# Three fused layers on one Trainium2 core: a first mixture whose TensorE order is written out, loads and splits in another order, and plain units weighed inside their additions

## The chip, the cores and the metric

The kernel runs on one core of a Trainium2 chip, all in fp32. The metric is the device time in microseconds (us) of one execution, lower is better. A core has a matrix engine (TensorE, PE in the profile; its weight loads are PEld), VectorE (DVE), ScalarE (ACT), GpSimd (POOL), and SyncE (SP), which here issues the large loads. Each engine works through its own queue in order; semaphores order the engines against each other.

## The reference

```python
# attention with a memory: B, H, S, D = 4, 8, 576, 64
scores = where(causal, -1e9, q @ k.T / sqrt(D)); a = softmax(scores)
q_p = where(q > 0, q, exp(q) - 1) + 1
mem_out = (q_p @ M_prev) / (q_p @ z_prev + 1e-6)
x = g * mem_out + (1 - g) * (a @ v)            # g from beta; x is 2304 x 512
# first mixture: 8 experts of 4 slots each
logits = x @ phi                               # 2304 x 32
slot_input = softmax(logits, axis=0).T @ x     # 32 x 512
for e in range(8):
    slot_out[e] = relu(slot_input[e] @ w1[e]) @ w2[e]      # 4 x 512 -> 4 x 1024 -> 4 x 512
x = softmax(logits, axis=1) @ slot_out
# second mixture: 8 experts over all rows, dense
P = exp(x @ w_gate - max); 8 rounds of row and column balancing of P
out = sum over e of P[:, e:e+1] * (relu(x @ w1[e]) @ w2[e])
```

## The kernel before

**Splitting.** Wherever TensorE multiplies in its fast form, an fp32 operand is split into a rounded part ("h", written by ScalarE) and a remainder ("l", operand minus rounded part, written by VectorE or GpSimd), and a product is three matmuls: h by h, h by l, l by h.

**Attention (0 to 257 us).** Sixteen pairs of heads, one after the other. Per pair the queries and keys are loaded split by head (`qd`, `kd`, two copies of 64 rows) and once more as a plain 128-row tile for the memory features (`qp`, `load_q1`); `qh`, `kh` and the remainders (`pre_ql`, `klz`) are made from `qd` and `kd`, and the features phi(q) = max(q, 0) + min(exp(q), 1) from `qp`. Then scores, row maxima, exponentials, transposes and the product with v. SyncE's queue issues the loads in the order in which the code calls them. What stands where on the engines in this stage is decided by the tile scheduler from costs, not written out.

**First mixture (273 to 316 us).** The x rows and the slot softmax are done by then. `sT` holds the 32 slot inputs; the weights come as 32 tiles `wm` of 1 MiB, 16 for layer 1 and 16 for layer 2. A block is four experts by 512 hidden columns: four `wm` tiles, each used by four 32-column matmuls (L830) into one bank `ph`, then a Relu into `h1`, then four transposes `phT` (L839) into `hT`. Layer 2 (L848) runs the same way over eight tiles a group into `pso`; `so` is its copy (L854, VectorE, 128x512) and `psT` its four transposes (L857) into `soT`, which is x's slot output for everything behind it. The combine weights c of one batch of rows are transposed with each block (`pc`, L809). The order on TensorE in this stage too is the scheduler's.

**Entry to the second mixture (316 to 324.5 us).** x is never formed: it is c times the 32 rows `soT`. `prepare_a` (L999, `pa`) multiplies soT by w1 of an expert; `spread_a` and `layer1` (L1052, `l`) give the hidden values of 256 rows (a "unit") at a time; `split_h` splits them into `a11`, `a21`, `a12`, `a22` (ACT L1082, DVE L1089). `w_hi` and `w_lo` (L963, L969) split the halves `raw` of w2 into BB1 and BB2, h and l. `gate_weights` writes `gsel`, with which `gate_scores` (L1159, `pgl`) makes the logits of the gate.

**Second mixture (324.5 us to the end).** Six plain units g = 0 to 5 (L1336) for expert 0, without the gate's weight since the gate is still being balanced (`balance_rows`, `sum_columns`, `balance_columns`); their results wait in `accA`, `accB`, `accD`. Then 66 units g = 6 to 71 in Strassen form: expert e and unit u from 0 to 8, seven products p1 to p7 each (L1369 to L1371), with sums `s1` to `s4` split beside them. The weights of each expert carry the gate's weight c from then on. The six plain units have to be multiplied by their gate weight `Pr` before expert 1 is added to them (units g = 9 to 14): `settle` does that with four VectorE multiplications per unit in g = 6 to 11. From 273 us's end on, that is from the entry to the second mixture, the order on PE, DVE, ACT and POOL is the order of the code: side work has a slot 7u + k, set by the tables `beside` and `at`, and is issued behind product k of unit u.

## Time and profile before

| | us |
|---|---|
| median of three runs | 1150.27 (1144.68 to 1154.06) |
| the profiled execution | 1150.16 |
| its span from first to last instruction | 1148.4 |
| TensorE matmuls busy | 1093.7 (95%) |
| VectorE, ScalarE, GpSimd busy | 873.3, 640.9, 659.4 |

The span is what the profile shows; the execution's own time is 1.8 us longer. Times of rows count from the span's start. Busy time of PE is modelled: matmuls overlap one another, so a row's duration is longer than the distance to the next.

### The profile page before, as it was taken

The numbers are of one execution on the slowest core, as the hardware profiler recorded it, in microseconds if no ns is written. First come the engines' busy times: TensorE is split into PE (matmuls) and PEld (weight loads), VectorE is DVE, ScalarE is ACT, GpSimd is POOL, SyncE is SP. The second block draws the span as 40 slices with busy tenths as digits, with TensorE's granted clock in tenths as the row PEclk, the third lists the DMA queues.
The fourth block names the chain that finished last, engine by engine and source line by source line (L and its number), as shares of the span: only waits on it lengthen the run. The fifth ranks groups of instructions, "written<-read, shape, count | busy, mean of one in ns | idle before, by whom it ended". The sixth has DMA issues, their size and how long they took to land.

```text
span 1148.4 us, 24410 instructions
## 1 busy us (share of the span) xinstructions
PE 1093.7 (95%) x9191; PEld 990.3 (86%) x9191; DVE 873.3 (76%) x1894; ACT 640.9 (56%) x1385; POOL 659.4 (57%) x602
## 2 busy tenths in 40 slices
PE   5899999998999999999999999999999999999998
PEld 4677777773377888899999999999999999999998
DVE  6788888875036568878778877877887887788876
ACT  6888878761233366455645644555464565456542
POOL 5333333300324287568767867786885777678665
PEclk9999999997989999999999999999999999999999
DMA  6677777338922003100400320130031013000111
GB/s 162 191 207 221 204 220 203 92 108 359 372 74 92 1 2 129 38 1 4 145 20 1 111 56 1 37 116 16 1 132 35 1 45 112 11 2 3 54 56 56
DMA packets 42789, 106.01 MB, mean 92 GB/s; under 512 B 8240, under 2 KB 18608, under 8 KB 38576
## 3 DMA queue, kind: packets, MB, share of 16 engines
q1 hardware_dynamic: 42240, 104.37, 28.4%
q8 instruction: 73, 1.20, 0.4%
q14 instruction: 44, 0.36, 0.1%
q10 hardware_dynamic: 432, 0.09, 0.0%
HBM read 96.04 MB, written 4.72 MB: 88 GB/s over the span
## 4 chain that ended last, share of the span: by engine, by line
PE 76%; DVE 14%; ACT 6%; issue 2%; DMA 1%; POOL 0%; SPq 0%; DVEq 0%; ACTq 0%
PE y L1369 16%; PE y L1371 16%; PE y L1370 16%; PE y L1336 5%; PE l L1052 5%; PE po L436 3%; DVE f L1076 2%; PE ph L830 2%; ACT sm L360 2%; PE pt L399 2%; PE pa L999 1%; PE pso L848 1%; DVE sm L356 1%; PE pc L1236 1%; PE pma L449 1%
## 5 line engine op out<-in xcount | busy, mean ns | idle before, releaser
L1076 DVE SCALAR_TENSOR_TENSOR f<-l,f 128x512 f32<-128x512 f32 x264 | 181.3, 687 | 57.4 <-ACT a11h L1082 49.4
L1093 POOL TENSOR_TENSOR s1l<-f,s1h 128x512 fp32r<-128x512 f32 x66 | 88.6, 1342 | 153.3 <-ACT s1h L1082 149.3
L1385 DVE TENSOR_TENSOR accA<-accA,y 128x512 f32<-128x512 f32 (+1 forms) x129 | 86.6, 671 | 41.1 <-PE y L1371 37.6
L1082 ACT ACTIVATE a12h<-l 128x512 fp32r<-128x512 f32 x72 | 43.3, 601 | 98.6 <-PE y L1371 82.3
L1093 POOL TENSOR_TENSOR s4l<-f,s4h 128x512 fp32r<-128x512 f32 x66 | 86.2, 1306 | 19.6 <-PE y L1370 10.4
L1385 DVE TENSOR_TENSOR accB<-accB,y 128x512 f32<-128x512 f32 x129 | 88.3, 685 | 5.0
L1093 POOL TENSOR_TENSOR s3l<-f,s3h 128x512 fp32r<-128x512 f32 x66 | 86.0, 1303 | 2.0 <-ACT s3h L1082 2.0
L1052 PE MATMUL l<-c4T,a 128*128 128x256 f32 x576 | 80.0, 282 | 6.9 <-DVE a22l L1089 6.0
L1093 POOL TENSOR_TENSOR s2l<-f,s2h 128x512 fp32r<-128x512 f32 x66 | 86.2, 1307 | 0.0
L360 ACT ACTIVATE sm<-sm,mn 128x128 f32<-128x128 f32 (+3 forms) x128 | 71.1, 556 | 19.6 <-DVE mn L356 17.9
L1052 PEld LDWEIGHTS l<-c4T,a 128*128 128x128 f32 x576 | 72.5, 190 | 9.9 <-DVE a22l L1089 8.3
L1072 ACT ACTIVATE f<-l 128x512 f32<-128x512 f32 x66 | 39.0, 592 | 72.8 <-PE l L1052 71.9
L1369 PE MATMUL y<-T2h,s2h 128*128 128x256 f32 x264 | 76.4, 289 | 0.0
L1369 PE MATMUL y<-T1h,s1h 128*128 128x256 f32 x264 | 73.4, 278 | 1.5 <-DVE accA L1385 1.5
L1369 PE MATMUL y<-BB1h,a11h 128*128 128x256 f32 x264 | 73.4, 278 | 1.1 <-DVE accB L1385 1.1
L969 POOL TENSOR_TENSOR BB1l<-raw,BB1h 128x512 fp32r<-128x512 f32 x32 | 41.1, 1300 | 57.8 <-ACT BB1h L963 53.6
L1370 PE MATMUL y<-BB2l,s4h 128*128 128x256 f32 x264 | 73.5, 278 | 0.4 <-DVE BB2l L969 0.3
L1369 PE MATMUL y<-BB2h,a12h 128*128 128x256 f32 x264 | 73.7, 279 | 0.0
L1371 PE MATMUL y<-BB1h,s3l 128*128 128x256 f32 x264 | 73.3, 278 | 0.1
L1370 PE MATMUL y<-T2l,s2h 128*128 128x256 f32 x264 | 73.3, 278 | 0.0
L1371 PE MATMUL y<-T2h,s2l 128*128 128x256 f32 x264 | 73.2, 277 | 0.0
L1371 PE MATMUL y<-BB1h,a11l 128*128 128x256 f32 x264 | 73.1, 277 | 0.0
(314 smaller groups left out, 4221.7 us busy)
## 6 DMA issues: line engine op xcount, KB each, us to landing
wm<-in_moe_w_dram SPq DMA_DIRECT2D x32, 1024.0 KB, 8.1
raw<-in_moe_w_dram SPq DMA_DIRECT2D x32, 512.0 KB, 3.9
w<-in_moe_w_dram SPq DMA_DIRECT2D x32, 512.0 KB, 4.3
qd<-in_q_dram SPq DMA_DIRECT2D x30, 288.0 KB, 4.3
kd<-in_k_dram SPq DMA_DIRECT2D x30, 288.0 KB, 4.5
qp<-in_q_dram SPq DMA_DIRECT2D x16, 288.0 KB, 3.6
vt<-in_v_dram SPq DMA_DIRECT2D x16, 256.0 KB, 2.8
out_dram<-accB SPq DMA_DIRECT2D x18, 128.0 KB, 1.8
```

The costliest lines, as they stand in the source:

```text
L360: nc.scalar.activation(out=sm[:, 0:n], in_=sm[:, 0:n], func=AF.Exp, scale=-1.0, bias=mnc, accum_out=X.sums[:, i, h : h + 1],)
L969: eng(g).tensor_tensor(out=w_tile(e, nm, "l")[:, h], in0=full(e, nm, i), in1=w_tile(e, nm, "h")[:, h].bitcast(F32), op=ALU.subtract,)
L1052: nc.tensor.matmul(ph[:, f, :], a4s[e][:, P * (KH * j + f) : P * (KH * j + f) + P], c4T[:, UT * u : UT * u + UT], start=True, stop=True,)
L1072: nc.scalar.activation(out=f_tile(g, nm), in_=ph(g, nm), func=AF.Relu)
L1076: nc.vector.scalar_tensor_tensor(out=f_tile(g, nm), in0=ph(g, src), scalar=0.0, in1=b, op0=ALU.max, op1=op)
L1082: nc.scalar.activation(out=h_tile(g, nm, "h"), in_=ph(g, nm) if a else FU[g, nm], func=AF.Relu if a else AF.Copy)
L1093: nc.gpsimd.tensor_tensor(out=lo, in0=FU[g, nm], in1=hi, op=ALU.subtract)
L1336: nc.tensor.matmul(Y[g, i], X[g, f"a{i}{j}", "hhl"[n]][:, f, :], BB[j, "hlh"[n]][:, f].rearrange("p a c -> p (a c)"), start=j == 1 and f = ...
L1369: nc.tensor.matmul(o_, hh[:, f, :], wh[:, f, :], start=f == 0, stop=False)
L1370: nc.tensor.matmul(o_, hh[:, f, :], wl[:, f, :], start=False, stop=False)
L1371: nc.tensor.matmul(o_, hl[:, f, :], wh[:, f, :], start=False, stop=f == KH - 1)
L1385: nc.vector.tensor_tensor(out=acc, in0=acc, in1=y, op=ALU.add)
```

## The change

1. **First pair.** The plain load `qp` of pair 0 is left out. Its features come from the split queries `qd`: two Exp on ScalarE and two maxima on VectorE, 64x576 each, in place of one Exp and one Relu of 128x576 on ScalarE. SyncE issues pair 1's queries, the memory, pair 1's keys and then v, where it issued `qp`, v, memory, queries, keys. In pair 1 one of the two query remainders moves from GpSimd to VectorE.
2. **First mixture.** TensorE's order is written by hand: layer 1 of a block runs whole, and the transposes of the block before stand behind it. Layer 2 of a group is in two halves, with transposes between them. The copy `so` is half VectorE, half ScalarE.
3. **Loads.** The four tiles of w1 are issued behind two of the four halves `raw` instead of behind all four.
4. **Splits of BB2.** The splits of B21 and B22 stand behind `a11`, `a21` and ahead of `gate_weights`; one of the two remainders of each moves from GpSimd to VectorE.
5. **Expert 1.** `prepare_a` two slots and `split_a`, `move_a` one slot later.
6. **Plain units.** `settle` is gone. For expert 1 and u below 6 the addition into `accB`, half of `accA` and `accD` multiplies by `Pr` as it adds (`weigh`).

```diff
         def load_q1(p):
             X = pairs[p]
             X.qp = e0.tile([P, NT * P], F32, tag="qp", name="qp", bufs=CFG["qpb"])
+            if p == 0:
+                return
...
         load_q1(0)
+        load_heads(1, "qd")
+        load_memory(0)
+        load_heads(1, "kd")
         load_v(0)
-        load_memory(0)
-        load_heads(1, "qd")
-        load_heads(1, "kd")
...
-                e or CFG["e_ql"][h], X.qh[sl, h, c0:c1], X.qd[sl, h, c0:c1], X.qh[sl, h, c0:c1]
+                e or ("DP" if X.p == 1 else CFG["e_ql"])[h], X.qh[sl, h, c0:c1], X.qd[sl, h, c0:c1], X.qh[sl, h, c0:c1]
...
+            if X.p == 0:
+                for h in range(2):
+                    sl = slice(D * h, D * h + D)
+                    nc.scalar.activation(out=X.qe[sl], in_=X.qd[sl, h], func=AF.Exp)
+                    nc.vector.tensor_scalar(
+                        out=X.qp[sl, 0:S], in0=X.qd[sl, h], scalar1=0.0, scalar2=None, op0=ALU.max
+                    )
...
+            if n:
+                so[g] = b2.tile([P, DM], F32, tag="so", name="so", bufs=1)
+                nc.vector.tensor_copy(so[g][:, 0:256], pso[g][:, 0:256])
+                nc.scalar.activation(out=so[g][:, 256:], in_=pso[g][:, 256:], func=AF.Copy)
...
+        with tc.manual_schedule(engines={mybir.EngineType.PE}):
+            c4 = combine(0)
+            first(0)
+            for bb in range(1, B):
+                first(bb)
+                first_t(bb - 1)
+                combine_t(bb - 1, c4)
+                c4 = combine(bb)
+            second(0, 0)
+            first_t(B - 1)
+            second(0, 1)
+            second(1, 0)
+            second_t(0)
+            second(1, 1)
+            combine_t(B - 1, c4)
+            second_t(1)
...
-    for u in range(RAW):
-        for i in range(4):
-            at(6 + u, 3 + i, settle, u, i)
...
+        def weigh(acc, T):
+            nc.vector.scalar_tensor_tensor(
+                out=acc, in0=acc, scalar=Pr[:, 2 * u + T, 0:1], in1=y, op0=ALU.mult, op1=ALU.add
+            )
...
-        if nm == "p5":
+        plain_before = e == 1 and u < RAW
+        if nm == "p5" and plain_before:
+            weigh(B_[:, 0:CW], 0)
+            weigh(B_[:, CW:], 1)
+        elif nm == "p5":
             put(halves(B_), both(y))
-        elif nm == "p1" and e == 1 and u < RAW:
+        elif nm == "p1" and plain_before:
             put(A[:, 0:CW], y, True)
-            put(A[:, CW:], y)
+            weigh(A[:, CW:], 0)
+        elif nm == "p7" and plain_before:
+            weigh(D_, 1)
...
-    load_raw(0)
+    load_raw(0, (0,))
     load_w1(0, 1)
+    load_raw(0, (1,))
...
-        for nm in ("B11", "B12", "B21", "B22"):
+        for nm in ("B11", "B12"):
             for i in range(2):
                 w_hi(0, nm, i)
                 w_lo(0, nm, i, "P")
...
         split_h(0, "a21")
+        for nm in ("B21", "B22"):
+            for i in range(2):
+                w_hi(0, nm, i)
+                w_lo(0, nm, i, "PD"[i])
         gate_weights()
```

How the instructions stand is shown at three places. The first is TensorE between the first two blocks of the first mixture, before: `ph_3940` is the second block's bank, `wm4` to `wm7` its tiles, `phT` and `pc` the transposes of the first block's hidden values and of the combine weights.

```order
L809 MATMUL pc_3912<-ident_67,c4_3890 128x128 x4
L809 MATMUL pc_3918<-ident_67,c4_3890 128x64
L830 MATMUL ph_3940<-wm4_1590,sT_65 32x512
L839 MATMUL phT_3921<-ident_67,h1_3910 128x128 x4
L830 MATMUL ph_3940<-wm4_1590,sT_65 32x512 x3
L830 MATMUL ph_3940<-wm5_1803,sT_65 32x512 x4
L830 MATMUL ph_3940<-wm6_2018,sT_65 32x512 x4
L830 MATMUL ph_3940<-wm7_2255,sT_65 32x512 x4
```

The same place on TensorE after the change, where `ph_3917` is the second block's bank.

```order
L841 MATMUL ph_3917<-wm4_1591,sT_65 32x512 x4
L841 MATMUL ph_3917<-wm5_1804,sT_65 32x512 x4
L841 MATMUL ph_3917<-wm6_2019,sT_65 32x512 x4
L841 MATMUL ph_3917<-wm7_2256,sT_65 32x512 x4
L852 MATMUL phT_3936<-ident_67,h1_3915 128x128 x4
L820 MATMUL pc_3942<-ident_67,c4_3895 128x128 x4
L820 MATMUL pc_3948<-ident_67,c4_3895 128x64
L841 MATMUL ph_3964<-wm8_2497,sT_65 32x512 x4
```

The single `ph` matmul that stood alone between two sets of transposes has joined the other three of its tile, and both sets of transposes now stand behind the whole block.

The second place is VectorE at the first unit's splits, before.

```order
L1089 SCALAR_TENSOR_TENSOR a11l<-l_4281,a11h 128x512
L1089 SCALAR_TENSOR_TENSOR a21l<-l_4281,a21h 128x512
L1147 TENSOR_TENSOR gsel<-pg,gsel 32x8 x2
L1150 TENSOR_TENSOR gsel<-ident 128x32
L1089 SCALAR_TENSOR_TENSOR a12l<-l_4276,a12h 128x512
L1089 SCALAR_TENSOR_TENSOR a22l<-l_4276,a22h 128x512
```

The same on VectorE after, where `raw_4223` and `raw_4225` are the second tiles of B21 and B22.

```order
L1125 SCALAR_TENSOR_TENSOR a11l<-l_4279,a11h 128x512
L1125 SCALAR_TENSOR_TENSOR a21l<-l_4279,a21h 128x512
L1005 TENSOR_TENSOR BB2l<-raw_4223,BB2h 128x2x256
L1005 TENSOR_TENSOR BB2l<-raw_4225,BB2h 128x2x256
L1183 TENSOR_TENSOR gsel<-pg,gsel 32x8 x2
L1186 TENSOR_TENSOR gsel<-ident 128x32
L1125 SCALAR_TENSOR_TENSOR a12l<-l_4274,a12h 128x512
```

Two remainders now stand ahead of `gsel` on VectorE. On ScalarE at the same place it is the four rounded parts of BB2, after the change:

```order
L1171 ACTIVATE soB<-soT 128x512
L1118 ACTIVATE a11h<-l_4279 128x512
L1118 ACTIVATE a21h<-l_4279 128x512
L999 ACTIVATE BB2h<-raw_4223 128x2x256 x2
L999 ACTIVATE BB2h<-raw_4225 128x2x256 x2
L1180 ACTIVATE gsel<-pg 128x8
L1118 ACTIVATE a12h<-l_4274 128x512
```

Before, `gsel` stood right behind `a21h` there; the four `BB2h` stood ahead of `ahi`, some rows earlier.

The third place is VectorE between units g = 9 and g = 10 (expert 1, u = 0 and 1), before.

```order
L1385 TENSOR_TENSOR accB<-accB,y_5564 128x512
L1221 TENSOR_TENSOR cP<-Cw,Pr 128x128
L1231 TENSOR_TENSOR c_5622<-cP,chi 128x4x64
L1385 TENSOR_TENSOR accA<-accA,y_5594 128x256
L1076 SCALAR_TENSOR_TENSOR f<-l_5612,f 128x512 x2
L1385 TENSOR_TENSOR accD<-accD,y_5627 128x256
L969 TENSOR_TENSOR BB2l<-raw_4783,BB2h 128x2x256
L1279 TENSOR_SCALAR accA<-accA,Pr 128x256
L1076 SCALAR_TENSOR_TENSOR f<-l_5607,f 128x512
L1089 SCALAR_TENSOR_TENSOR a11l<-l_5612,a11h 128x512
L1279 TENSOR_SCALAR accB<-accB,Pr 128x256
L1385 TENSOR_TENSOR accA<-accA,y_5655 128x512
```

The same place on VectorE after.

```order
L1415 SCALAR_TENSOR_TENSOR accB<-accB,Pr,y_5558 128x256 x2
L1257 TENSOR_TENSOR cP<-Cw,Pr 128x128
L1267 TENSOR_TENSOR c_5617<-cP,chi 128x4x64
L1415 SCALAR_TENSOR_TENSOR accA<-accA,Pr,y_5588 128x256
L1112 SCALAR_TENSOR_TENSOR f<-l_5606,f 128x512 x2
L1415 SCALAR_TENSOR_TENSOR accD<-accD,Pr,y_5622 128x256
L1005 TENSOR_TENSOR BB2l<-raw_4789,BB2h 128x2x256
L1112 SCALAR_TENSOR_TENSOR f<-l_5601,f 128x512
L1125 SCALAR_TENSOR_TENSOR a11l<-l_5606,a11h 128x512
L1411 TENSOR_TENSOR accA<-accA,y_5650 128x512
```

The multiplications L1279 between the sums `f` and the splits `a` are gone; the one addition of 128x512 into `accB` has become two of 128x256, and those into `accA` and `accD` keep their number.

## Rows read from the trace of the kernel before

**Rows 1.** Window, attention: length, busy us (count) of PE PEld DVE ACT POOL, PEclk, DMA.
```profile
31.50:257.00 225.50, 207.82 (x1866) 168.67 (x1864) 195.05 (x686) 180.38 (x485) 67.98 (x109) 1.00 0.63 184
```

**Rows 2.** Windows: a piece, units 6 to 12, units 15 to 21; columns as above.
```profile
412.50:425.00 12.50, 11.43 (x96) 10.92 (x95) 10.97 (x14) 7.25 (x15) 12.50 (x10) 1.00 0.00 1
408.73:499.79 91.06, 81.88 (x695) 78.13 (x694) 76.67 (x118) 51.16 (x102) 64.05 (x50) 1.00 0.16 53
520.64:598.96 78.32, 78.32 (x696) 77.09 (x695) 63.29 (x104) 43.81 (x84) 57.64 (x46) 1.00 0.19 62
```

**Rows 3.** Waits of PE from 408.73 to 499.79: total us, times, longest.
```profile
PE l L1052 <- DVE a22l L1089: 5.5, 6, 1.2
PE y L1369 <- DVE accA L1385: 1.5, 2, 1.2
```

**Rows 4.** Line L1279, settle: duration ns min/median/max, first and last start.
```profile
L1279 DVE TENSOR_SCALAR accB<-accB,Pr x12: 335/640/1449, 419.0 to 488.2; 128x256 f32<-128x256 f32 x12
L1279 DVE TENSOR_SCALAR accA<-accA,Pr x6: 537/1265/1475, 416.4 to 483.3; 128x256 f32<-128x256 f32 x6
L1279 DVE TENSOR_SCALAR accD<-accD,Pr x6: 339/1352/1416, 424.1 to 489.6; 128x256 f32<-128x256 f32 x6
```

**Rows 5.** Groups of DVE from 408.73 to 499.79: count, busy us, mean ns.
```profile
L1385 DVE TENSOR_TENSOR accB<-accB,y 128x512 f32<-128x512 f32 x11 | 7.4, 676 | 0.1
...
L1385 DVE TENSOR_TENSOR accD<-accD,y 128x256 f32<-128x256 f32 x10 | 4.1, 409 | 0.0
```

**Rows 6.** Timeline of PE, one block of the first mixture: start, length.
```profile
284.42 0.86 PE L809 MATMUL pc<-ident,c 128*128 128x128 f32 x5
285.21 1.05 PE L830 MATMUL ph<-wm,sT 128*32 128x512 f32 x2
286.18 0.66 PE L839 MATMUL phT<-ident,h 128*128 128x128 f32 x4
286.77 3.63 PE L830 MATMUL ph<-wm,sT 128*32 128x512 f32 x30
290.33 0.86 PE L809 MATMUL pc<-ident,c 128*128 128x128 f32 x5
```

**Rows 7.** Timeline, end of the first mixture: start, length, idle before and what ended it.
```profile
305.67 2.43 ACT L963 ACTIVATE BB1h<-raw 128x512 fp32r<-128x512 f32 x4 [8.01 <-DMA raw<-in_moe_w_dram]
...
307.12 7.07 PE L848 MATMUL pso<-wm,hT 128*32 128x512 f32 x64
...
308.37 2.29 ACT L963 ACTIVATE BB2h<-raw 128x512 fp32r<-128x512 f32 x4 [0.27 <-DMA raw<-in_moe_w_dram]
...
315.10 0.63 PE L857 MATMUL psT<-ident,so 128*128 128x128 f32 x4 [0.91 <-DVE so L854]
...
316.05 1.93 PE L999 MATMUL pa<-w,soT 128*32 128x256 f32 x32 [0.32 <-DVE soT L858]
```

**Rows 8.** Timeline behind the first layer1: the splits, gsel and pgl.
```profile
324.56 0.60 ACT L1082 ACTIVATE a21h<-l 128x512 fp32r<-128x512 f32 x1 [0.76 <-DVE a11l L1089]
...
325.89 0.34 DVE L1147 TENSOR_TENSOR gsel<-pg,gsel 32x8 fp32r<-32x8 f32 x2
...
327.66 1.48 PE L1159 MATMUL pgl<-gsel,c4T 128*128 128x40 f32 x12
```

**Rows 9.** Tile BB2l on DVE: duration ns min/median/max.
```profile
L969 DVE TENSOR_TENSOR BB2l<-raw,BB2h x7: 1462/1470/1552, 457.0 to 1057.9; 128x512 fp32r<-128x512 f32 x7
```

**Rows 10.** Windows in which the granted clock is half.
```profile
24.01:30.84 6.83, 6.09 (x27) 4.06 (x29) 1.38 (x8) 4.63 (x13) 3.25 (x5) 0.50 0.05 13
...
320.97:327.80 6.83, 6.71 (x25) 6.04 (x25) 2.67 (x7) 2.35 (x5) 0.00 (x0) 0.50 0.57 231
```

**Rows 11.** Timeline of PE at expert 1's prepare_a.
```profile
349.98 1.93 PE L999 MATMUL pa<-w,soT 128*32 128x256 f32 x32 [1.42 <-DVE cs L1207]
```

**Rows 12.** Timeline, first pairs: the remainders on POOL and PE's wait.
```profile
20.20 2.63 POOL L258 TENSOR_TENSOR qh<-qd,qh 64x512 fp32r<-64x512 f32 x2
...
22.88 0.44 PE L354 MATMUL ps<-kh,qh 128*128 128x128 f32 x2 [2.30 <-POOL qh L258]
```

More of the change, by code (lines that the diff above doesn't have):

```diff
@@ L306, in pre_exp @@
             X.qe = e5.tile([P, S], F32, tag="sc", name="qe")
[L307 to L308 removed]
+            if X.p == 0:
[5 more added lines that the diff above has]
+                    )
+            else:
+                nc.scalar.activation(out=X.qe, in_=X.qp[:, 0:S], func=AF.Exp)
+                nc.scalar.activation(out=X.qp[:, 0:S], in_=X.qp[:, 0:S], func=AF.Relu)
             nc.gpsimd.memset(X.qp[:, S:], 0.0)
@@ L816, in combine_t @@
                 )
-        hTs = []
-        for g in range(E // 4):
-            hT = b2.tile([P, KF, 4 * SPE + 32 - SPE], F32, tag="hT", name="hT")
+        hTs = [b2.tile([P, KF, 4 * SPE + 32 - SPE], F32, tag="hT", name="hT") for _ in range(2)]
+        for hT in hTs:
             nc.gpsimd.memset(hT[:, :, 4 * SPE :], 0.0)
-            hTs.append(hT)
-            for n in range(FF // 512):
-                bb = FF // 512 * g + n
-                c4 = combine(bb)
-                ph = ps_h.tile([P, 512], F32, tag="h", name="ph")
-                for c in range(KD):
-                    for j in range(4):
-                        e = SPE * (4 * g + j)
-                        nc.tensor.matmul(
-                            ph[32 * j : 32 * j + 32, :], sT[:, c, e : e + 32], wm[1, g, n, c][:, j, :],
-                            start=(c == 0), stop=(c == KD - 1),
-                        )
-                h1 = b2.tile([P, 512], F32, tag="h1", name="h1", bufs=1)
-                nc.scalar.activation(out=h1, in_=ph, func=AF.Relu)
-                combine_t(bb, c4)
-                pt = ps_m.tile([P, 512], F32, tag="m", name="phT")
-                for c in range(4):
-                    nc.tensor.transpose(pt[:, P * c : P * c + P], h1[:, P * c : P * c + P], ident)
-                nc.vector.tensor_copy(
-                    hT[:, 4 * n : 4 * n + 4, 0 : 4 * SPE].rearrange("p c (j s) -> p c j s", j=4),
-                    pt.rearrange("p (c j s) -> p c j s", c=4, j=4)[:, :, :, 0:SPE],
-                )
@@ L844, in infini_attention_soft_moe_sinkhorn_moe, with first @@
-        for g in range(E // 4):
-            pso = ps_g.tile([P, 512], F32, tag="g", name="pso")
-            for f in range(KF):
+        NN = FF // 512
+        h1s, pso, so = {}, {}, {}
+        def first(bb):
+            g, n = divmod(bb, NN)
+            ph = ps_h.tile([P, 512], F32, tag="h", name="ph")
+            for c in range(KD):
+                for j in range(4):
+                    e = SPE * (4 * g + j)
+                    nc.tensor.matmul(
+                        ph[32 * j : 32 * j + 32, :], sT[:, c, e : e + 32], wm[1, g, n, c][:, j, :],
+                        start=(c == 0), stop=(c == KD - 1),
+                    )
+            h1 = h1s[bb] = b2.tile([P, 512], F32, tag="h1", name="h1", bufs=1)
+            nc.scalar.activation(out=h1, in_=ph, func=AF.Relu)
@@ new lines, in first_t, with second @@
+        def first_t(bb):
+            g, n = divmod(bb, NN)
+            pt = ps_m.tile([P, 512], F32, tag="m", name="phT")
+            for c in range(4):
+                nc.tensor.transpose(pt[:, P * c : P * c + P], h1s[bb][:, P * c : P * c + P], ident)
+            nc.vector.tensor_copy(
+                hTs[g][:, 4 * n : 4 * n + 4, 0 : 4 * SPE].rearrange("p c (j s) -> p c j s", j=4),
+                pt.rearrange("p (c j s) -> p c j s", c=4, j=4)[:, :, :, 0:SPE],
+            )
+        def second(g, n):
+            if n == 0:
+                pso[g] = ps_g.tile([P, 512], F32, tag="g", name="pso")
+            for f in range(KF // 2 * n, KF // 2 * n + KF // 2):
@@ L914, in w_tile, with load_raw @@
         return W[e, nm, z]
-    def load_raw(e):
-        for r, c in ((0, 0), (0, 1), (1, 0), (1, 1)):
+    def load_raw(e, rows=(0, 1)):
+        for r, c in ((r, c) for r in rows for c in (0, 1)):
             t = rawq[e, r, c] = mC.tile([P, KH, CW], F32, tag=f"raw{r}{c}", name=f"raw{r}{c}")
@@ L1273, in add_u @@
         eng(g[1]).tensor_tensor(out=D_, in0=D_, in1=A[:, 0:CW], op=ALU.add)
-    def settle(u, i):
-        A, B_, D_ = accA[:, u], accB[:, u], accD[:, u]
-        t, T = ((A[:, CW:], 0), (B_[:, 0:CW], 0), (B_[:, CW:], 1), (D_, 1))[i]
-        nc.vector.tensor_scalar(
-            out=t, in0=t, scalar1=Pr[:, 2 * u + T, 0:1], scalar2=None, op0=ALU.mult
-        )
     def at(u, k, f, *args):
```

16 lines of the change are left out of this document (7 added, 9 removed).

## The prediction

> **What bounds the kernel now.** I read the busy time by stage first, then PE's waits in the stages where it is not full, then the timeline of those places. PE is the bound nearly everywhere, so a microsecond counts only where PE stands still. In units 15 to 21 PE is busy for 78.32 of 78.32 us; in units 6 to 12, which are the same seven units (u = 6, 7, 8, 0 to 3) one expert earlier, it takes 91.06 us with the same number of matmuls [rows 2]. Attention leaves 225.5 - 207.8 = 17.7 us of PE idle, in many short waits [rows 1]. The first mixture has PE and the loads close together; its cost is in how it ends [rows 6, 7]. The change touches all of these.
>
> **Part 6, settle: -10.5 (range -8 to -11.5).** The excess of units 6 to 12 is 91.06 - 78.32 = 12.74 us. Of it PE's waits for VectorE's `a22l` take 5.5 and for `accA` 1.5 [rows 3]; the rest is in PE's busy time, which is 81.88 against 78.32 although the matmuls are equally many: a matmul that starts late behind another's modelled end shows no idle, and each restart costs a fill. What keeps VectorE late is in rows 4: 24 multiplications by their medians, 12 x 0.640 + 6 x 1.265 + 6 x 1.352 = 23.4 us, in a stretch where VectorE is busy 76.67 us against 63.29 in the later one [rows 2]. They stand between the sums and the splits that PE waits for. All are removed. What is put in their place is one operation more per unit, since two additions of 128x256 at 409 ns replace one of 128x512 at 676 ns: 2 x 0.409 - 0.676 = 0.14 us a unit, 0.85 us over g = 9 to 14 on VectorE, with over 10 us of VectorE now free there, so nothing on PE [rows 5]. Not all of the excess is settle's: one of the six `a22l` waits comes ahead of the first settle at 416.4 [rows 3, 4], and a few short ones are for weights or c. I keep 2.2 us for these, one longest wait of 1.2 and as much again less a little. 12.74 - 2.2 = 10.5. The small end is the sum of the waits alone, 5.5 + 1.5 and about 1 for `accB`, 8; the large end, 11.5, leaves one wait of 1.2 us standing.
>
> Rows 4 also show why this costs more than its size: the same 128x256 multiplication takes 0.335 us or up to 1.45. The Trainium skill, SBUF — State Buffer, section Who interferes with whom, says that such a scalar multiplication can take the port pair that VectorE shares with GpSimd, and that whoever comes second is blocked for the whole instruction, while an operation with one SBUF input does not contend; by it the new fused additions, which read y from PSUM, stay near 0.41 us. The additions of rows 5 agree.
>
> **Part 5, prepare_a of expert 1: -1.5 (range -0.5 to -1.8).** PE stands 1.42 us ahead of `pa` for `cs`, which has to leave the one bank that both use [rows 11]. Two slots later fourteen plain matmuls stand between, so this wait and the restart behind it go. Smaller waits of the balancing stay.
>
> **Parts 2 and 3, first mixture: -4.0 at `pa` (range -3 to -4.1).** One block takes 290.33 - 284.42 = 5.91 us: combine transposes 0.79, two `ph` records 0.97, `phT` 0.59, the other thirty 3.56 [rows 6]. Unsplit, 32 records cost 32 x 7.07 / 64 = 3.54 by layer 2's rate [rows 7], so a block costs 0.79 + 0.59 + 3.54 = 4.92: 1.0 saved, four times (three in layer 1, one in layer 2) = 4.0. The waits for `so` ahead of `psT`, 0.91 each and two of them [rows 7], now have matmuls or the last combine transposes over them; half of the last one may stay. PE would be ready for `pa` at 316.05 - 4.0 - 0.9 = 311.1 or so. But `pa` needs all four tiles of w1. ScalarE waited for raw tile 1 until 305.67 and for raw tile 3 until 308.37 [rows 7], 1.35 us a tile of half a MiB at most. With the old order w1's last tile is the eighth, at 305.67 + 7 x 1.3 = 314.8; with the new one the sixth, at about 312.1. So `pa` starts at 312.1, not 311: 316.05 - 312.1 = 4.0. The load order is what makes the gain; without it some 1.3 would be left.
>
> **Part 4, splits of BB2 ahead of the gate: +2.0 (range +0.7 to +3.3).** Before, `a21h` ends at 325.16 on ScalarE and `gsel` is written by 326.4 on VectorE (two rows of 0.34 together from 325.89, and a last small one of some 0.2); `pgl` starts at 327.66 behind seven plain matmuls, so there is 1.2 us of slack [rows 8]. After, all four `BB2h`, 2.29 us [rows 7], come first on ScalarE: 327.45. Behind them VectorE splits two remainders, the first from about 326.3, the second from 327.8, each as long as the trace shows this operation, 1.47 us [rows 9]: 329.2; then `gsel` with 0.5: 329.8. `pgl` is 2.1 late. What is queued behind `gsel` on VectorE is `a12l`, `a22l` and the gate's chain, which PE needs only later. All these times come 4.0 earlier with the mixture; the relation stays. With the free price of an equal addition, 0.68 [rows 5], `gsel` would come at 328.7 and `pgl` only 1.0 late. I take the long price, since all seven rows of this operation have it and GpSimd does the other two remainders at the same time.
>
> The Trainium skill, SBUF — State Buffer, section Who interferes with whom, speaks against this edit: it says that a VectorE operation with two SBUF inputs contends with a GpSimd operation that reads SBUF. Rows 9 bear it out, and by it part 4 costs 2.0 instead of about 1.0.
>
> **Clock: +1.0 (range 0 to +3).** From 320.97 to 327.80 the granted clock is 0.50, the lower level of 1.2 GHz, with PE nearly full in it [rows 10]. A new stop of 2 us at its end can keep the low level for longer. PE would then take up to twice as long over the next few microseconds; I take 1.0 as part of the 3.4 us (half of 6.83) that the present stretch costs. Mixture, gate and clock together: -4.0 + 2.0 + 1.0 = -1.0 (range -3.5 to +1.5).
>
> **Part 1, first pair: -1.5 (range -4 to +0.5).** PE waits 2.30 us at 22.88 for pair 1's query remainders, two on GpSimd, 2.63 us together [rows 12]; behind it the clock is at the low level from 24.01 to 30.84 [rows 10]. With one of the two on VectorE that wait can shrink by 1.3, and pair 1's loads come one to three microseconds earlier because `qp` and v are out of their way. If the clock stays up as well, up to 3.4 more would be won. Against it VectorE gets two maxima of 64x576 in pair 0; their price is not shown, the nearest are 0.41 of the 128x256 addition [rows 5] and 1.35 of the held multiplication [rows 4]; 0.45 each, 0.9 together, on the path of pair 0's first maxima. I take 1.3 + 1.1 - 0.9 = 1.5 won, where 1.1 is a third of what the clock could give.
>
> **Attention elsewhere: 0 (range -1.5 to +1.5).** The scheduler also shifts rows of VectorE, ScalarE and GpSimd in many pairs, while PE's order hardly changes. Nothing in the trace tells the sign; the range is a tenth of the 17.7 us.
>
> **Sum.** -10.5 - 1.5 - 1.0 - 1.5 = -14.5. The profiled execution took 1150.16, 0.1 from the median, so 1150.2 - 14.5 = 1135.7, **1136**.
>
> **Rivals.**
> - The front parts give nothing: `pgl` late, the low clock for 3 us more, no gain in the first pair. Then +1 in place of -1 in the mixture and 0 in place of -1.5: 1150.2 - 10.5 - 1.5 + 1 = 1139.2. For it speaks that each edit there adds work to VectorE or ScalarE at a waiting place.
> - GpSimd becomes the bound in units 6 to 8. It is busy 12.50 of 12.50 us from 412.5 to 425 [rows 2], on ten splits and sums of 1.25, and a unit without settle would take 78.32 / 7 = 11.2. If ten are still due per unit, two such units lose 1.3 each, and late splits then hold the next: half of the gain goes, 1141. Against it: over units 6 to 12 GpSimd is busy only 64 of 91 us, and its queue is empty at times right behind.
> - Slower: the scheduler's new order in attention lets PE wait for a remainder as at 22.88, 2.30 us [rows 12], in pair after pair. Seven pairs of sixteen make up for the whole gain; eight cost 18.4: 1154. Against it: PE's order stays, and VectorE has 30 us free in this stage [rows 1].
> - The load order doesn't do what it says: if the eight half-MiB tiles move at once and not in turn, w1 lands near 314.8 as before and the mixture wins 1.3, not 4.0: 1138.5.
>
> **How the numbers follow.** Forecast 0.60, GpSimd 0.13, nothing in front 0.17, loads 0.05, slower 0.05. All good ends at once, -11.5 - 1.8 - 3.5 - 4 - 1.5 = -22.3, would give 1128; 1127 is put just under it. The high end, 1146, takes in half of settle's gain with nothing in front (1150.2 - 5.3 - 1 + 2). About 1% (11.5 us) is what a measurement of this kernel can tell from no change: faster means under 1138.8. The forecast's own spread puts 0.85 of its 0.60 there, the others 0.10 together: 0.61. Slower than 1161.8 needs eleven such pairs: 0.03. The rest, 0.36, is same.
>
> **What would show it.** Units 6 to 12 in some 80 us with PE's waits for `a22l` and `accA` gone; `pa` starting near 312 less what the start won; a wait of PE ahead of `pgl` of about 2 us; no wait of PE ahead of the second `pa`; a shorter or absent half-clock stretch near 25 us. Wrong would make it: new waits of PE for GpSimd's `s` tiles in units 7 and 8, a low clock well past `pgl`, or an attention stage longer than 227 us.

## The result and the profile after

The changed kernel takes 1138.3 us (median of four runs, 1135.8 to 1142.6) against 1149.85 for the kernel before (four runs, 1144.7 to 1154.1). That is 11.5 us between the two medians. The ratio of the runs is 0.9905, interval 0.9877 to 0.9932, so 0.95% or some 11 us faster. A second set of four runs of the same kernel gave 1141.5 and a ratio of 0.991 (0.9875 to 0.9945). The forecast was 1136, the range 1127 to 1146.

The profiled execution of the changed kernel took 1135.8 us with a span of 1133.6, 14.8 below the span before. First the windows, with the columns of [rows 1]: attention, units 6 to 12, units 15 to 21, and the two pieces behind the first `l` in which the clock is low.

```profile
31.50:257.00 225.50, 206.44 (x1850) 167.32 (x1848) 192.51 (x684) 178.38 (x480) 68.80 (x108) 0.99 0.63 183
405.23:487.43 82.20, 79.14 (x696) 76.72 (x695) 59.77 (x98) 50.91 (x102) 63.30 (x50) 1.00 0.18 59
508.28:586.51 78.23, 78.06 (x696) 76.78 (x695) 63.27 (x104) 43.79 (x84) 57.58 (x46) 1.00 0.19 62
312.88:319.68 6.80, 6.76 (x23) 5.56 (x23) 3.05 (x4) 3.82 (x8) 2.09 (x2) 0.50 0.49 193
322.98:329.80 6.82, 6.82 (x22) 5.66 (x22) 0.95 (x3) 1.60 (x3) 2.57 (x2) 0.50 0.01 2
```

Units 6 to 12 take 82.20 us where they took 91.06 [rows 2], with VectorE busy 59.8 us instead of 76.7. Units 15 to 21 are unchanged. PE's waits in units 6 to 12, as [rows 3]:

```profile
PE pc L1272 <- DVE c L1267: 1.5, 1, 1.5
PE l L1088 <- DVE a22l L1125: 0.8, 2, 0.6
PE pa L1035 <- ACT c4T L1277: 0.3, 1, 0.3
PE y L1395 <- ACT accD L1409: 0.2, 1, 0.2
```

The waits for `accA` and `accB` are gone and those for `a22l` are down from 5.5 to 0.8. One wait is new in its place, 1.5 us for `c` in unit 7; before, PE waited 0.4 us for `c`, in unit 9. The fused additions have these prices (groups of VectorE, as [rows 5]):

```profile
L1415 DVE SCALAR_TENSOR_TENSOR accB<-accB,Pr,y 128x256 f32<-128x256 f32 x8 | 3.5, 476 | 0.0
...
L1415 DVE SCALAR_TENSOR_TENSOR accD<-accD,Pr,y 128x256 f32<-128x256 f32 x4 | 1.9, 472 | 0.0
```

In the first mixture a block of layer 1 now runs in one piece (timeline of PE, against [rows 6]): it repeats after 283.68 - 278.88 = 4.80 us, where it was 5.91.

```profile
278.88 3.64 PE L841 MATMUL ph<-wm,sT 128*32 128x512 f32 x32
282.45 0.66 PE L852 MATMUL phT<-ident,h 128*128 128x128 f32 x4
282.94 0.80 PE L820 MATMUL pc<-ident,c 128*128 128x128 f32 x5
283.68 3.64 PE L841 MATMUL ph<-wm,sT 128*32 128x512 f32 x32
```

PE's waits from the end of the mixture to `pgl`, total us, times, longest, against [rows 7, 8]:

```profile
PE pgl L1195 <- DVE gsel L1186: 2.8, 1, 2.8
PE p L1061 <- DVE alo L1046: 0.9, 1, 0.9
...
PE pa L1035 <- DMA w<-in_moe_w_dram: 0.7, 1, 0.7
```

The stop ahead of `pgl` is there; before, it was none. What stands ahead of `gsel` is seen in the timeline of the other engines:

```profile
316.84 2.18 ACT L999 ACTIVATE BB2h<-raw 128x512 fp32r<-128x512 f32 x4
...
317.59 2.95 POOL L1005 TENSOR_TENSOR BB2l<-raw,BB2h 128x512 fp32r<-128x512 f32 x2 [6.27 <-issue]
318.01 3.08 DVE L1005 TENSOR_TENSOR BB2l<-raw,BB2h 128x512 fp32r<-128x512 f32 x2 [0.34 <-ACT BB2h L999]
318.92 0.16 ACT L1180 ACTIVATE gsel<-pg 128x8 fp32r<-128x8 f32 x1
...
321.11 0.34 DVE L1183 TENSOR_TENSOR gsel<-pg,gsel 32x8 fp32r<-32x8 f32 x2
321.46 0.80 DVE L1186 TENSOR_TENSOR gsel<-ident 128x32 fp32r<-128x32 f32 x1
...
322.41 2.14 PE L1195 MATMUL pgl<-gsel,c4T 128*128 128x40 f32 x12 [2.76 <-DVE gsel L1186]
```

VectorE's two remainders take 1.54 us each beside GpSimd's, and even the small constant half of `gsel` takes 0.80 where it took some 0.2. The wait of 1.42 us at expert 1's `pa` [rows 11] is gone. In the first pairs PE no longer waits 2.30 us for `qh` [rows 12]; it waits 1.31 for `kh` there, and then 1.36 for `klz` where it was 1.2.

The first expert's `pa` is cut in two by w1, which lands while it runs (timeline of PE, against [rows 7]):

```profile
306.17 1.15 PE L1035 MATMUL pa<-w,soT 128*32 128x256 f32 x6 [0.32 <-DVE soT L877]
307.98 1.91 PE L1035 MATMUL pa<-w,soT 128*32 128x256 f32 x26 [0.66 <-DMA w<-in_moe_w_dram]
```

The next table gives stages of all profiles, in us, from the first PE row of each stage to that of the next; one execution each. "attention" is the start of the last pair's `po`; "units 6-12" the seven units, "rest" from unit 13 to unit 70; "low" the whole microseconds behind `pa` in which the granted clock was about half.

| kernel | attention | ph to pa | pa to l | l to pgl | pgl to unit 6 | units 6-12 | rest | low |
|---|---|---|---|---|---|---|---|---|
| before | 254.3 | 42.7 | 5.0 | 6.6 | 81.1 | 91.1 | 625.2 | 321-327 |
| changed | 252.5 | 35.5 | 6.7 | 9.5 | 82.8 | 82.2 | 622.9 | 313-319, 323-329 |
| after_again | 251.6 | 37.7 | 7.3 | 9.5 | 81.3 | 82.2 | 627.3 | 313-323, 327-330 |
| weigh_alone | 252.9 | 43.8 | 5.0 | 4.6 | 81.1 | 81.6 | 627.8 | none |
| mix_alone | 253.3 | 36.8 | 9.8 | 6.6 | 81.3 | 91.0 | 631.4 | 316-326 |
| pair_old | 253.8 | 37.8 | 6.5 | 8.7 | 82.6 | 82.2 | 627.3 | 326-332 |
| loads_old | 251.6 | 37.6 | 8.6 | 8.6 | 82.7 | 82.5 | 628.0 | 326-332 |
| bb2_old | 252.5 | 37.1 | 8.0 | 6.6 | 82.4 | 81.6 | 625.8 | 316-329 |
| bb2_pool | 255.2 | 38.0 | 7.2 | 7.4 | 83.0 | 82.2 | 625.1 | 317-334 |
| bb2_late | 255.2 | 37.6 | 6.5 | 5.4 | 81.2 | 81.6 | 626.2 | 327-330 |
| sel_early | 251.7 | 38.4 | 6.0 | 8.7 | 83.1 | 82.2 | 622.8 | 314-331 |
| late_pool | 253.1 | 37.2 | 6.9 | 6.4 | 79.9 | 82.5 | 624.0 | 317-323 |
| gate_free | 249.3 | 36.9 | 7.1 | 4.4 | 79.7 | 82.2 | 624.5 | none |

One more sum of the table's columns is used below, from the first `ph` to unit 6: 135.4 us before, 134.6 and 135.9 in the two profiles of the changed kernel, 134.5 in mix_alone, 130.7 in bb2_late, 130.4 in late_pool and 128.1 in gate_free. And since w1 can cut `pa` in two, the mixture is also measured to the end of `pa`: from the first `ph` that is 44.6 us before, 39.2 and 40.0 in the changed kernel, 43.2 in loads_old and 41.2 in mix_alone.

### The profile page after: what moved, and what is told of

Read it like the earlier page. It is cut to its first block, busy times and chain, and to the rows that moved or that the text cites. A ratio compares the mean times of both kernels' runs of the same rounds, so it can differ in the third digit from the quotient of the medians.

```text
span 1133.6 us, 24388 instructions
## 1 busy us (share of the span) xinstructions
PE 1083.4 (96%) x9191; PEld 985.7 (87%) x9191; DVE 864.5 (76%) x1881; ACT 640.4 (56%) x1387; POOL 656.5 (58%) x599
## 4 chain that ended last, share of the span: by engine, by line
PE 72%; DVE 12%; ACT 7%; DMA 6%; issue 2%; POOL 0%; SPq 0%; DVEq 0%; ACTq 0%; POOLq 0%
PE y L1395 16%; PE y L1396 16%; PE y L1397 16%; PE y L1362 5%; PE l L1088 5%; PE po L447 3%; DMA kd<-in_k_dram 2%; ACT sm L371 2%; DMA w<-in_moe_w_dram 2%; DMA wm<-in_moe_w_dram 2%; PE pt L410 1%; PE pa L1035 1%; DVE f L1112 1%; DVE sm L367 1%; PE pc L1272 1%
## 5 line engine op out<-in xcount | busy, mean ns | idle before, releaser
L1411 DVE TENSOR_TENSOR accA<-accA,y 128x512 f32<-128x512 f32 x123 | 84.1, 684 | 38.6 <-PE y L1397 37.9
L1411 DVE TENSOR_TENSOR accB<-accB,y 128x512 f32<-128x512 f32 x123 | 84.3, 685 | 4.4
L1005 POOL TENSOR_TENSOR BB1l<-raw,BB1h 128x512 fp32r<-128x512 f32 x32 | 41.3, 1304 | 57.9 <-ACT BB1h L999 57.9
L1395 PE MATMUL y<-BB2h,s4h 128*128 128x256 f32 x264 | 73.1, 277 | 0.2 <-ACT accD L1409 0.2
L1395 PE MATMUL y<-BB1h,s3h 128*128 128x256 f32 x264 | 73.0, 277 | 0.0
L1396 PE MATMUL y<-BB1l,s3h 128*128 128x256 f32 x264 | 73.0, 277 | 0.0
```

The lines of the kernel that those rows point to most:

```text
L1005: eng(g).tensor_tensor(out=w_tile(e, nm, "l")[:, h], in0=full(e, nm, i), in1=w_tile(e, nm, "h")[:, h].bitcast(F32), op=ALU.subtract,)
L1395: nc.tensor.matmul(o_, hh[:, f, :], wh[:, f, :], start=f == 0, stop=False)
L1396: nc.tensor.matmul(o_, hh[:, f, :], wl[:, f, :], start=False, stop=False)
L1411: nc.vector.tensor_tensor(out=acc, in0=acc, in1=y, op=ALU.add)
```

## The experiments

The theory after the result: settle carries the gain (8.9 us); the mixture's order and the loads win some 5 by the end of `pa`, and nearly all of that is given back between there and the first units, by remainders and casts on VectorE that GpSimd holds, and by the clock. The rivals: the first mixture and the first pair carry the gain as well, or the give-back is the clock's alone.

**Part 6 alone.** The kernel before, with part 6 of the diff above, of which this is the beginning and the end:

```diff
-    for u in range(RAW):
-        for i in range(4):
-            at(6 + u, 3 + i, settle, u, i)
...
+        elif nm == "p7" and plain_before:
+            weigh(D_, 1)
```

> The kernel before with part 6 alone (settle gone, the additions weigh). Theory: settle's 23 us on VectorE made PE's waits for a22l, accA and accB in units 6 to 12; without it these seven units take 82 to 83 us in place of 91.06, all times up to unit 6 stay, and the whole gains 8 to 9 us, the larger part of the changed kernel's gain. Rival, GpSimd is the bound there: the seven units stay at 86 us or more and the gain is 5 or less.

Measured: 1142.5 against 1150.6, ratio 0.9941 (0.9919 to 0.9964): 6.8 us, with an interval of 4 to 9. The seven units take 81.58 us (91.06 before), in this row of its windows:

```profile
406.72:488.30 81.58, 79.13 (x696) 76.90 (x695) 57.80 (x98) 51.07 (x102) 63.57 (x50) 1.00 0.18 59
```

9.5 us are won there, a little more than the timed runs show: their interval ends at 9.3. The rival falls: GpSimd is busy 64 us in either kernel and does not become the bound.

**Parts 2 and 3 alone.** The kernel before, with the mixture's order as in the changed kernel and this load order:

```diff
-    load_raw(0)
+    load_raw(0, (0,))
     load_w1(0, 1)
+    load_raw(0, (1,))
```

> The kernel before with parts 2 and 3 alone (mixture order and load order; settle, the splits ahead of prepare_a, part 1 and part 5 as before). Theory: from the first ph to pa it takes 37 to 38 us where it was 42.7, units 6 to 12 take 91 us again, PE waits 1.4 us ahead of expert 1's pa again, and there is no stop ahead of pgl; the whole gains 3 to 5 us, some 1146. Rival: the loads hold pa, so ph to pa stays above 40 us.

Measured: 1152.3 against 1151.6, ratio 0.9992 (0.9969 to 1.0015): nothing. The expected gain at `pa` is there, 36.8 us from `ph` where it was 42.7, so the loads don't hold its start at 40; but w1 then holds `pa` itself for 1.2 us. The expected 3 to 5 us are not there. From `pa` to the first `l` it takes 9.8 us instead of 5.0, as the waits of PE from 268 to 410 us show:

```profile
PE p L1051 <- DVE alo L1036: 2.5, 1, 2.5
PE pa L1025 <- DVE cs L1233: 1.4, 1, 1.4
PE pa L1025 <- DMA w<-in_moe_w_dram: 1.2, 2, 0.7
```

ScalarE's `BB2h` stands ahead of `ahi` there, and its raw tiles now land behind w1, as ScalarE's timeline shows:

```profile
313.12 2.32 ACT L989 ACTIVATE BB2h<-raw 128x512 fp32r<-128x512 f32 x4 [2.37 <-DMA raw<-in_moe_w_dram]
...
315.35 0.36 ACT L1034 ACTIVATE ahi<-pa 128x256 fp32r<-128x256 f32 x1
```

So the splits of BB2 can't stay ahead of `ahi` with this order of the loads; bb2_old below shows that part 4's place for them costs as much. My expectation was too high by this term; the rest of the program is also 6 us longer in this execution than in that of before, of which more below.

**The old load order** in the changed kernel:

```diff
-    load_raw(0, (0,))
+    load_raw(0)
     load_w1(0, 1)
-    load_raw(0, (1,))
```

> The changed kernel with the old load order, all four raw tiles ahead of w1's four. Theory: w1 is then the last to land and pa waits for it; PE's wait for w1 ahead of pa is 2 to 4 us where it was 0.66, and the kernel is 2 to 3 us slower than the changed one, some 1141. Rival: the late raw tiles cost as much in the changed order, through the splits of BB2, and the time stays.

Measured: 1145.9 against 1150.2, ratio 0.996 (0.9935 to 0.9985). By the medians of the same session that is 4.4 us worse than the changed kernel's second set, by the ratios some 6, and the intervals of the second set and of this run overlap. PE's waits for w1 are 1.8 us in three pieces inside `pa`, not 2 to 4 ahead of it. Its last piece:

```profile
312.60 1.91 PE L1035 MATMUL pa<-w,soT 128*32 128x256 f32 x26 [0.62 <-DMA w<-in_moe_w_dram]
```

So `pa` ends 43.2 us behind the first `ph` (271.30), 4.0 and 3.2 later than in the two profiles of the changed kernel, and 1.4 sooner than before. Up to the first `l` it is 4.0 and 1.2 later, since in the second profile of the changed kernel the casts into `sel` and the low clock take 2 us back (below). This agrees with the forecast 2 to 3 in size; the two profiles are too far apart to tell it more closely. The rival falls.

**The first pair as before** in the changed kernel:

```diff
-            if p == 0:
-                return
...
-        load_heads(1, "qd")
-        load_memory(0)
-        load_heads(1, "kd")
         load_v(0)
+        load_memory(0)
+        load_heads(1, "qd")
+        load_heads(1, "kd")
...
-                e or ("DP" if X.p == 1 else CFG["e_ql"])[h], ...
+                e or CFG["e_ql"][h], ...
...
-            if X.p == 0:
+            if False:
...
```

> The changed kernel with part 1 undone (plain load of the first pair's queries, Relu on ScalarE, the old order of the first loads, both query remainders of pair 1 on GpSimd). Theory: part 1 gains nothing that lasts; the last pair's po starts between 252 and 256 as in the kernels with it, and the time is that of the changed kernel, 1138, within 3 us. Rival: part 1 is worth the 1.7 us seen in the first profile; then PE's wait of 2.3 us for qh of pair 1 is back, and po of the last pair starts at 254.3 or later.

**The changed kernel once more**, no edit.

> The changed kernel once more, unaltered, for a second trace. Theory: where and for how long the granted clock is low near 23 to 31, 263 to 279 and behind the first layer1 differs from one execution to the next of the same kernel, so the first profile's gain of 1.7 us in the first pairs and its early rise at 268 are chance. Then one of these stretches stands elsewhere or has another length here, and the last pair's po starts anywhere from 252 to 256. Rival: they belong to the code; then po of the last pair starts within 0.3 us of 252.54 and the low stretches are those of the first profile.

Measured: pair_old 1145.1, ratio 0.9952 (0.9931 to 0.9974); after_again 1141.5, ratio 0.991 (0.9875 to 0.9945). The last pair starts its `po` at 249.3 to 255.2 in the nine profiles with part 1 (mean 252.5) and at 252.9 to 254.3 in the four without (mean 253.6). The low stretch of [rows 10] near 24 stands there in some profiles of the same code and not in others: the changed kernel has none before 70, after_again none before 57, bb2_pool and bb2_late, with the same first pairs, have it at 23 to 30. So the 1.8 us of the first profile lies within what one execution differs from the next. But all four profiles without part 1 have that low stretch, and five of the nine with it have none. In pair_old the wait of 2.3 us for `qh` is back, as its rival said, while its last `po` at 253.8 lies within the theory's range; the forecast time, 1138 within 3 us, was missed. By the ratios, undoing part 1 costs 4.8 to 5.4 us with intervals that touch or overlap; by the medians of the same session it is 3.6; the traces show about 1. How much part 1 is worth stays open between them.

**The place of the splits of BB2.** Six kernels vary parts of the stretch between `pa` and `pgl`, all from the changed kernel. bb2_pool leaves the place and takes VectorE out:

```diff
-                w_lo(0, nm, i, "PD"[i])
+                w_lo(0, nm, i, "P")
```

> The changed kernel with all four remainders of BB2 on GpSimd, their place unchanged. Theory: VectorE's two remainders (1.54 us each) hold gsel back and the stop of 2.76 us ahead of pgl lets the clock fall once more (323.0 to 329.6). Then the stop shrinks to under 0.5 us, the second low stretch is gone, and the second mixture starts 5 to 6 us earlier: some 1132. Rival, the four rounded parts on ScalarE are what gsel waits for: the stop stays at 1.5 us or more and the low stretch with it. Second rival, the low stretch has another cause than the stop: only 2.5 us are won.

bb2_late moves the loop behind the gate's weights; late_pool does both:

```diff
         split_h(0, "a21")
+        gate_weights()
         for nm in ("B21", "B22"):
             for i in range(2):
                 w_hi(0, nm, i)
                 w_lo(0, nm, i, "PD"[i])
-        gate_weights()
```

> The changed kernel with the splits of B21 and B22 behind gate_weights. Theory: gsel comes at once, no stop ahead of pgl, no second low stretch, 5 to 6 us won against the changed kernel, some 1132; a12l and a22l come later but PE needs them only some 17 matmuls behind pgl. Rival: the stop moves to the first matmul with a12 or BB2, 2 us or more, and half of the gain is lost.

> The changed kernel with the third edit alone: the splits of B21 and B22 behind gate_weights, all four remainders on GpSimd. Theory: no stop of over 1.3 us ahead of pgl, which comes 5 to 5.5 us behind the start of the first l; p still waits 2 us for alo behind the held casts; units 0 to 5 begin some 4 us earlier than in the changed kernel and the time is 1133 to 1136. Rival: the low clock comes from the stop between pa and l and stays; then the time is 1138.

bb2_old undoes part 4 (`for nm in ("B11", "B12", "B21", "B22")` ahead of `prepare_a`):

> The changed kernel with part 4 undone: all splits of BB1 and BB2 ahead of prepare_a again, the load order as changed. Theory: ScalarE's parts of BB2 wait for the last raw tile (landed at 310.4) and stand ahead of ahi, so ahi and the first l come 1.5 us later, but the stop ahead of pgl and the second low stretch are gone: 3 to 4.5 us better than the changed kernel, some 1134, and 1.5 worse than with the splits behind the gate. Rival: without part 4 the late tiles of raw cost as much as the stop, and the time is that of the changed kernel, 1138.

sel_early leaves the splits and moves two other pieces of VectorE's work:

```diff
-        nc.vector.tensor_copy(
-            sel[:, :, 32 * r : 32 * r + 32], ident.rearrange("p (j s) -> p j s", j=4)
-        )
+        nc.scalar.activation(
+            out=sel[:, :, 32 * r : 32 * r + 32], in_=ident.rearrange("p (j s) -> p j s", j=4),
+            func=AF.Copy,
+        )
...
     def gate_slots():
+        nc.vector.tensor_tensor(
+            out=gsel[:, E:], in0=ident[:, 0:32], in1=ident[:, 64:96], op=ALU.add
+        )
...
-        nc.vector.tensor_tensor(
-            out=gsel[:, E:], in0=ident[:, 0:32], in1=ident[:, 64:96], op=ALU.add
-        )
```

> The changed kernel with two of the three edits of the further version: the casts into sel on ScalarE and the constant half of gsel ahead of the first layer1; the splits of B21 and B22 stay ahead of the gate, two remainders on VectorE. Theory: the chain BB2h on ScalarE, BB2l on VectorE sets pgl whatever PE does, so pgl stays some 8 us behind the start of the first l (9.5 at the low clock, 8.6 at the high one, less 0.6 for the constant half), PE's stop ahead of it is 2 to 4 us, the clock is low behind it and the time is 1137 to 1140. Rival: the held casts were the main cost; then most of the further version's gain is here, 1134 or less.

gate_free has the edits of sel_early and late_pool together:

> A further version: the changed kernel with the splits of B21 and B22 behind gate_weights and their remainders on GpSimd, the three casts into sel on ScalarE, and the constant half of gsel written ahead of the first layer1. Theory: what VectorE does on two SBUF operands or as a cast beside GpSimd's splits is held (sel casts 1.3 us where 0.2 when free, the constant half of gsel 0.7 to 0.9 where 0.19); with none of it ahead of alo and gsel, PE's waits ahead of p and pgl fall to about 0.9 and under 0.2 us, 2 to 3 us better than the changed kernel, and up to 3 more if the clock then stays up: 1132 to 1136. Rival: the clock decides, and these waits only fill a stretch that is low anyway; then the time is within 2 us of the changed kernel's.

| kernel | median us | ratio to before | interval | PE's stop ahead of p | ahead of pgl |
|---|---|---|---|---|---|
| changed | 1138.3 | 0.9905 | 0.9877 to 0.9932 | 0.9 | 2.8 |
| changed, second set | 1141.5 | 0.991 | 0.9875 to 0.9945 | 2.1 | 2.8 |
| bb2_pool | 1139.1 | 0.9885 | 0.9848 to 0.9922 | 2.1 | 0.6 |
| bb2_late | 1138.3 | 0.9902 | 0.9875 to 0.9929 | 1.8 | 1.3 |
| bb2_old | 1140.4 | 0.9907 | 0.9877 to 0.9936 | 2.5 | none |
| sel_early | 1138.2 | 0.9889 | 0.9857 to 0.9922 | 2.0 | 1.9 |
| late_pool | 1134.6 | 0.9838 | 0.9807 to 0.9869 | 0.9 | none |
| gate_free | 1133.0 | 0.9848 | 0.9819 to 0.9877 | 0.9 | 0.4 |

Taking VectorE out alone, or moving the loop alone, gives no gain that the timed runs can tell; both together give 6.5 to 7.7 us by the ratios, and the two kernels that have both are the best, with intervals that end where the changed kernel's begins. The traces divide it otherwise: from the first `ph` to unit 6 bb2_late, which only moves the loop, takes 130.7 us and late_pool 130.4, against 134.6 and 135.9 in the changed kernel. So moving the loop looks like the larger part, and what taking VectorE out adds isn't shown; four runs of bb2_late, from 1135.2 to 1142.2, can't settle it.

In bb2_pool the stop ahead of `pgl` fell to 0.6, near what was forecast, but the clock was low from 317 to 334, as long as in any profile, and ate it: in this one execution the second rival of that run held. In bb2_late a stop of 1.3 stayed, since the constant half of `gsel` took 0.94 us beside GpSimd, and the stop of its rival, at `a12` or BB2, didn't come. In late_pool the constant half took 0.95 as well; its profile has no stop because the clock was low from 317 to 323, and PE's plain matmuls covered it.

bb2_old went as its rival said, no better than the changed kernel; in sel_early the stop ahead of `pgl` stayed, and the one ahead of `p` too, since ScalarE did the casts in 0.71 us but then `BB1h`, 2.17 us, ahead of `ahi`; so the held casts were not the main cost. Nor did they cost late_pool the 2 us ahead of `p` that I expected: it was 0.9, with PE held by w1 before. Whether the two edits of sel_early add anything to late_pool isn't shown: its interval and gate_free's overlap almost wholly.

gate_free's waits, as above:

```profile
PE p L1062 <- DVE alo L1047: 0.9, 1, 0.9
PE l L1089 <- DVE a L66: 0.9, 1, 0.9
...
PE pgl L1196 <- ACT BB2h L999: 0.4, 1, 0.4
```

and its window from the first `l` to unit 6, at the high clock throughout:

```profile
312.56:396.63 84.07, 82.83 (x427) 66.70 (x428) 46.57 (x114) 34.76 (x77) 33.82 (x27) 1.00 0.14 49
```

In the changed kernel the same stretch takes 405.23 - 312.88 = 92.35 us. gate_free beats both kernels: 17 us or 1.5% below the one before, and by the ratios some 7 below the changed one.

## Why the prediction was right, and where it was off

**Total.** Forecast -14.5, timed -11.5. The first profile shows -14.8 in its span: -1.8 up to the last pair's `po`, -0.9 from there to the first `ph`, -0.8 from there to unit 6, -8.9 in units 6 to 12 and -2.3 in "rest". The last is no doing of the change: from unit 13 on the code is the same, and "rest" came out 2.1 us longer in the second profile. That the first profile's sum hits the forecast is therefore luck in part. Ahead of unit 6 the traces look more like the first rival of the prediction, in which the front parts give nothing (1139.2), than like its own sum: `pgl` late, 3.1 us lost to the low clock behind it in the first profile, no sure gain in the first pair. The median, 1138.3, lies between 1136 and that rival, nearer to the rival.

**Part 6, settle: the mechanism was right, the term mis-sized.** Forecast -10.5 (range -8 to -11.5), measured -8.9 in both profiles of the changed kernel and -9.5 alone. The new additions took 0.47 to 0.48 us each, all 24 of them, where 0.41 was forecast, and none was held. I kept 2.2 us of the excess for waits that aren't settle's; 3.9 stay in the changed kernel (82.2 - 78.3). Most of the difference is one wait in unit 7 that I hadn't counted: 1.5 us for `c`, or, where that is absent, 1.2 for `accD`. The wait for `c` comes from a row whose length I had not reckoned with:

```profile
419.17 1.29 POOL L1129 TENSOR_TENSOR s3l<-f,s3h 128x512 fp32r<-128x512 f32 x1
419.89 3.21 DVE L1257 TENSOR_TENSOR cP<-Cw,Pr 128x128 f32<-128x128 f32 x1
...
420.43 1.28 POOL L1129 TENSOR_TENSOR s4l<-f,s4h 128x512 fp32r<-128x512 f32 x1
421.68 1.27 POOL L996 TENSOR_TENSOR ft<-raw,ft 128x512 f32<-128x512 f32 x1
```

`cP` reads two tiles of SBUF and takes some 0.5 us elsewhere (the median of its 37 times in this profile); here it waits through three of GpSimd's operations that follow one another without a gap and ends 0.15 us behind the last. So the second rival had a grain of truth: GpSimd's full stretch does cost, though not as a bound but by holding VectorE. Where the stretch fell otherwise (weigh_alone, bb2_late, bb2_old) the wait for `c` is gone, a wait of 1.2 us for `accD` takes its place, and the units take 81.6; so the held `cP` itself costs 0.6.

**Part 5: right, as far as other runs tell.** No run undoes it alone. -1.5 forecast; "pgl to unit 6" at the high clock throughout is 81.1 with the old place (weigh_alone, and before, whose low stretch ends at `pgl`) and 79.7 with the new one (gate_free): -1.4.

**Parts 2 and 3: the mechanism right, the landing of w1 mis-sized.** Forecast -4.0 at `pa`, bounded by w1's landing at 312.1, which is 38.8 us behind the first `ph` (273.34). The start of `pa` came out at -7.2 and -5.0 from there, but the forecast was for a `pa` that starts with all of w1 at hand, and the rows of the first profile show that it did not: six matmuls ran at 306.17, and the other 26 waited until 307.98, which is 37.3 us behind the first `ph` at 270.65. To its end `pa` gained 5.4 and 4.6 us. With the old load order the bound was forecast at 314.8, 41.5 behind `ph`, leaving a gain of 1.3; in loads_old w1 released `pa` 41.3 behind `ph`, and the gain is 1.4. So w1 is the bound, as forecast, and the load order is worth 3 to 4 us of the gain; the mis-sized term is its landing in the new order, 1.4 us early in the first profile. Why it came earlier there stays open. Blocks shrank by 1.1 us as worked out (1.0).

**Part 4 and the clock: the mechanism was right, the price too low.** Forecast +2.0 for `pgl` and +1.0 for the clock. From the first `l` to `pgl` it is +3.0 in both profiles, at the low clock as before, and +4.0 at the high clock (8.6 in loads_old, 8.7 in pair_old, against 4.6 in weigh_alone). The chain of `BB2h` on ScalarE and two remainders on VectorE sets `pgl` whatever PE does: where PE was at the low clock its seven plain matmuls covered a part and the stop was 2.8; in pair_old and loads_old, at the high clock, the same chain left a stop of 4.6 us and the clock was low behind it, from 326 to 332. This is the stop in loads_old:

```profile
PE pgl L1195 <- DVE gsel L1186: 4.6, 1, 4.6
```

I had worked out the slack from a trace at the low clock and so got half of the cost at the high one. Of the 1.0 us missing at the low clock, 0.6 is the constant half of `gsel`, 0.80 long where I had taken 0.2. Behind `pgl` the low stretch cost 82.8 - 79.7 = 3.1 us in the first profile and 1.6 in the second. Not foreseen was the stretch from `pa` to `l`, +1.7 and +2.3. In the first profile all of it is w1's cut in `pa` shown above: from the end of `pa` to `l` it takes 3.0 us where it took 3.1, and the casts into `sel` end before `ahi` does. In the second profile w1 doesn't cut `pa`, and the casts, which with the shorter mixture fall beside GpSimd's splits of BB1, hold `alo` until 312.97, while the clock is low from 313:

```profile
308.93 5.26 POOL L1005 TENSOR_TENSOR BB1l<-raw,BB1h 128x512 fp32r<-128x512 f32 x4 [39.92 <-ACT BB1h L999]
309.02 2.29 PE L1035 MATMUL pa<-w,soT 128*32 128x256 f32 x32 [0.32 <-DVE soT L877]
309.40 3.64 DVE L1021 CAST sel<-ident 128x128 fp32r<-128x128 f32 x3
311.35 0.38 ACT L1044 ACTIVATE ahi<-pa 128x256 fp32r<-128x256 f32 x1 [0.95 <-PE pa L1035]
...
312.97 0.41 DVE L1046 TENSOR_TENSOR alo<-pa,ahi 128x256 fp32r<-128x256 f32 x1
313.43 0.58 PE L1061 MATMUL p<-ahi,sel 128*128 128x256 f32 x1 [2.12 <-DVE alo L1046]
```

Three casts take 3.64 us; in weigh_alone, where GpSimd's work had ended just ahead of them, they took 0.22 each (duration in ns, min/median/max):

```profile
L985 DVE CAST sel<-ident x3: 219/219/228, 316.4 to 316.6; 128x128 fp32r<-128x128 f32 x3
```

Mixture, gate and clock came to +0.6 and +1.9 together where -1.0 was forecast (range to +1.5; the high ends of its three parts add up to +3.3). That nearly all of the mixture's gain is given back is shown by the stretch from the first `ph` to unit 6, 134.6 and 135.9 us where it was 135.4 with part 5's wait still in it, and by bb2_late, late_pool and gate_free, whose traces are 5 to 7 us shorter there than before. mix_alone, whose ratio is 0.9992, gives it back in another way, by `BB2h` ahead of `ahi`.

**Part 1 and attention.** -1.5 and 0 forecast; -1.8 in the first profile, with pairs 3 to 15 all shifted by 1.6 to 1.8 but two. The other profiles show that a single execution can't tell this from chance. The rival of slow pairs didn't come. One sum in its price is off: eleven waits of 2.30 us make 1161.0, and it takes twelve to pass 1161.8.
